# A pair's activations in one run of columns, four single blocks before the second half's weights, and one count of a search step on ScalarE

## The chip, the cores and the metric

The kernel runs as one program on one core of a Trainium2 chip. The metric is device time in microseconds (us). TensorE (PE) multiplies, VectorE (DVE), ScalarE (ACT) and GpSimd (POOL) work elementwise, SyncE (SP) and GpSimd issue the DMAs.

## The reference

Three layers stand one behind the other: attention over pooled keys, a layer with a rational function between two products, and a mixture of eight experts with a greedy assignment. N = 4608 tokens, width 512.

```python
# attention: 8 batches, 8 heads, 576 tokens, width 64; keys and values are means over 8 tokens
k_p, v_p = mean8(k), mean8(v)
x = softmax(q @ k_p.T / 8) @ v_p                 # [4608, 512]
# rational layer, inner width 2048
h = x @ w_in
P = a[0] + a[1]*h + a[2]*h*h + a[3]*h*h*h
Q = 1 + abs(b[0])*abs(h) + abs(b[1])*h*h
y = (P / (Q + 1e-6)) @ w_out                     # [4608, 512]
# experts: all pairs (token, expert) in falling order of their logit; a token takes the first
# expert that still has room (cap = 576)
logits = y @ w_gate
assigned = greedy(logits, cap=576)
for e in range(8):
    out[assigned == e] = relu(y[assigned == e] @ w1[e]) @ w2[e]
```

## The kernel before, in words

All operations are recorded first in an `Order`: each has an engine, an assumed duration, what it reads and writes, and a priority (its place in the recording, or a large negative number for the routing). `Order.run` then plays the list through with these durations and writes out the instructions of each engine in the order that comes of it. So the order on an engine is fixed when the program is built, and an instruction at the head of an engine's queue that waits holds up all behind it.

Every factor of a product is split into a high and a low part (`xh`, `xl`; `wih`, `wil`; `woh`, `wol`; `hi`, `lo`), and each product is three matmuls.

Phase 1 does attention and the rational layer for 18 blocks of 256 tokens. The inner width is worked in two halves of 1024, each in four pieces of 256 (`fp` 0 to 3). In the first half the blocks 0 to 3 go singly (twice, for two pieces each) and the blocks 4 to 17 in pairs; in the second half the blocks 0 and 1 go singly, the rest in pairs. A step is 512 columns of `h`: one pair and 128 inner features, or one block and 256. In a step PE makes `h` (`mm_h`, line 693), ACT and DVE and POOL make the rational function (`act1`, `act2`, lines 708 to 735), and PE multiplies by `w_out` (`mm_y`, lines 791 to 794); the output of 128 tokens gathers over all steps of a part. `hi` and `lo` of a step wait for these products in a ring of buffers `mgl`: five (`mg`), and five more (`mgx`, opened by `swap_m`, closed by `swap_b`) while the first half has pairs.

Attention for the blocks is recorded between the steps. `x` of four blocks lies in SBUF in two tiles, `xt[0]` and `xt[1]`, of [128, block, 4, 256]; a pair's matmul reads two runs of 256 columns, 1024 columns apart. Each block's `x` is stored to DRAM (`store_x`) and loaded again for the second half (`load_b`, line 884, issued on POOL): blocks 0 and 1 into `xt[0]`, which the first half's last pair (16, 17) uses, and blocks 2 and 3 into a new tile `xhr`, `xlr`.

The second half's weights come as 64-bit numbers in 16 parts and are turned into float32 and split (`prep_w`: ACT line 409, DVE 410 to 414, PE 432 and 436, POOL 345). They start when attention is done and its memory is given back (`closed`, from the step after block 15): one part with each step. The tiles of pieces 2 and 3 are those of the first half's pieces 0 and 1, and so are filled once that half is over.

For the last four blocks of the second half the output products are held back (`late`, `DEFER`) and fill PE while the first expert is chosen: 8 groups of 24 matmuls of 512 columns, each followed by ACT line 832 and POOL line 833.

Phase 2 takes the experts one after the other. `route(k)` finds which expert is next and which tokens it takes; its core is `search`, ten steps that narrow a threshold by a factor of four, each with three counts of keys at or above a candidate (`count`, line 1290, DVE), a transpose, a sum and two small operations, all on DVE. Then come gathers on POOL (`fetch`), transposes (`turn`, line 1630) and the expert's two products (`ffn`). `route(0)` stands between the phases; `route(k+1)` runs beside `ffn(k)`.

Of the kernel before, what the change touches and what calls it, by code (L numbers as in the profile page):

```python
# [25 lines left out]
NT = B * S  # L26
DM = H * D
DFF = 2048
E = 8
# [18 lines left out]
GBUFS, MGX, GDX = 5, 5, 5  # L48
# [12 lines left out]
for _name, _width in (("wr", E), ("J", 4), ("sel", E), ("ones", 128), ("qmask", 4), ("cmask", 32), ("own", 2), ("triu", 128), ("s1", 5),  # L61
                      ("tcol", 36), ("pcol", 2), ("rtri", E * E)):
    RC[_name] = (RC.get("n", 0), RC.get("n", 0) + _width)
    RC["n"] = RC[_name][1]
# [15 lines left out]
class Part:  # L80
# [5 lines left out]
    def __call__(self):  # L86
        return self.buf()[:, self.j]

# [202 lines left out]
class Kern:  # L291
# [163 lines left out]
    def init_att(self):  # L455
# [21 lines left out]
        self.xt = [tuple(b(p, [128, 2, 4, BLK], F32R, f"{x}{k}") for x in ("xh", "xl")) for k, p in enumerate(("xp", "xq"))]  # L477
        self.xb = [tuple(Part(x, k % 2) for x in self.xt[k // 2]) for k in range(XBUFS)]
# [201 lines left out]
    def mm_h(self, st):  # L680
# [198 lines left out]
    def load_b(self, n):  # L879

        s, j = n // 2 % 2, n % 2
        extra = [("xr", m) for m in range(NB) if m % XBUFS == j] if n < 2 else []
        for k, x in enumerate(self.x1[s]):
            self.op("Pool", 1.05, lambda k=k, x=x: self.nc.gpsimd.dma_start(x()[:, j], self.x_d[n]()[:, k]), r=[("xd", n, k)],
                    w=[("xs", s, j, k)] + extra, nbytes=524288)

    def phase1(self):
# [4 lines left out]
        for p in ("wp", "mp", "xp", "xq", "ap"):  # L892
# [24 lines left out]
        pieces = {h: [(h, fp, k) for fp in range(NFP) for k in range(4)] for h in range(2)}  # L917
        loads = {h: list(pieces[h]) for h in range(2)}
# [19 lines left out]
        parts = alone + [(0, [n], range(NFP)) for n in range(SPLIT, PAIRS)] + [(0, [n, n + 1], range(NFP)) for n in range(PAIRS, NB, 2)]  # L938
# [11 lines left out]
        for i, st in enumerate(steps):  # L950
            st["i"] = i
            n = st["blk"]
            if st["half"] == 0:
# [4 lines left out]
                if n == SPLIT and st["first"] and st["half"] == 0:  # L958
                    self.swap_m()
                while done < needed[st["blks"][-1]]:  # L960
# [8 lines left out]
                elif not closed and NB - 3 in xdone:  # L969
                    closed = True  # L970
                    reads = [k for k in self.g.lastw if self.in_pool(k, ("ap", "xq"))]
                    reads += [("xr", m) for m in range(NB) if m % XBUFS > 1] + [("x", m, s, k) for m in self.xkeys for s in range(2) for k in self.xkeys[m]]
                    def swap():
                        self.close("ap")
                        self.close("xq")
# [4 lines left out]
                    for fp in range(2):  # L980
                        self.w_tiles(1, fp, "wpb", f"b{fp}")
                        for t in self.w[1, fp]:
                            for k in range(4):
                                self.g.lastw[t, k] = self.g.lastw["swap"]
                    self.staging("raw1")
# [4 lines left out]
                if closed and pieces[1] and pieces[1][0][1] < 2:  # L990
# [3 lines left out]
            else:  # L994
                if st["first"] and n == 0:
# [8 lines left out]
                    for fp in (2, 3):  # L1004
                        self.w[1, fp] = self.w[0, fp - 2]
                while pieces[1] and pieces[1][0][1] <= st["fp"]:
                    piece(1)
# [5 lines left out]
                st["x"] = x if len(st["blks"]) == 2 else tuple(Part(t, n % 2) for t in x)  # L1013
# [81 lines left out]

    def free_x(self, s):
# [3 lines left out]
        new = [tuple(View(x, lambda t, j=j, i=i: t[:, j].rearrange("p (i c) t -> p i (c t)", i=2)[:, i]) for i in range(2))  # L1100
# [5 lines left out]
    def swap_b(self):  # L1106

        def swap():
            self.close("mx")
# [4 lines left out]
        self.op("Z", 0.0, swap, w=[k for k in self.g.lastw if self.in_pool(k, ("wq", "stg", "mx"))] + ["swapb"])  # L1114
        self.mgl = [g for g in self.mgl if g[0].pool != "mx"]
        x = tuple(self.buf("yp", [128, 2, 4, BLK], F32R, x) for x in ("xhr", "xlr"))
        self.x1 = [self.xt[0], x]
        for j in range(2):
            for k in range(2):
                self.g.lastw["xs", 1, j, k] = self.g.lastw["swapb"]  # L1120
# [16 lines left out]
    def swap_g(self):  # L1137
# [5 lines left out]
        self.more_g("gd", "swapg", GDX, "gd")  # L1143
        more = self.ring(MORE_R, "gd", [128, 2 * BLK], F32, "mrg")
# [27 lines left out]
    def init_route(self):  # L1172
# [40 lines left out]
        self.cand, self.thr = b("rt", [128, 4], F32, "cand"), b("rt", [128, 3], F32, "thr")  # L1213
# [73 lines left out]
    def count(self, D, key, cand, col, ck):  # L1287

        j = self.BJ[col % 2]
        D(.43, lambda: self.nc.vector.tensor_scalar(  # L1290
            j(), key(), cand(), None, op0=ALU.is_ge, op1=ALU.add, accum_out=self.cnt()[:, col:col + 1]),
# [22 lines left out]
    def search(self, D, key, col, steps, cap, between=None, sole=None):  # L1314
# [4 lines left out]
        (base, bk), (J, jk) = self.small(0, 4), self.small(4, 4)  # L1319
        D(.07, lambda: V.tensor_scalar(cand(), J(), float(4 ** (steps - 1)), None, op0=ALU.mult), r=[jk], w=[cand])  # L1320
        for i in range(steps):
# [9 lines left out]
            D(.14, lambda Y=Y: V.scalar_tensor_tensor(self.njunk()[:, 0:3], Y()[:, 0:3], cap() if callable(cap) else cap, self.own(3),  # L1331
# [494 lines left out]
```

## Time and profile before

| what | us |
|---|---|
| runs (three), median | 1531.73 (1530.3 to 1533.25) |
| the profiled execution | 1529.58 |
| its span, first to last instruction | 1527.8 |
| PE busy in the span | 1454.1 |
| DVE, ACT, POOL busy | 1097.6, 883.3, 865.0 |

The profile shows one execution. Busy time is the time in which an engine has at least one instruction under way; matmuls overlap, so the distance from one start to the next says more than a matmul's own duration. PEclk and "granted clock" give the share of TensorE's full clock of 2.4 GHz that was granted; 0.5 is its lower level, 1.2 GHz. "Waits" put an engine's idle time down to what ended it.

### The profile page before, as it was taken

What the parts mean: (1) busy time and instruction counts of PE and PEld (TensorE: products, weight loads), DVE (VectorE), ACT (ScalarE), POOL (GpSimd) and SP (SyncE); (2) the same over time, 40 slices, a digit from 0 to 9 for tenths busy, and PEclk for the clock granted to TensorE, in tenths of its full rate; (3) what the DMA queues carried; (4) which work ended last, traced back from release to release, by engine and by line L of the source; (5) the groups of instructions that cost most, each with busy time, mean ns of one, the idle gap of its engine ahead of it and who ended that gap; (6) DMA issues with size and microseconds to landing.
All of it is one profiled execution on the core that took longest, in us unless ns stands there. A gap on an engine that the chain in (4) does not pass through costs nothing. (4 is left out here: it accounts for less than half of the span.)

```text
span 1527.8 us, 27162 instructions
## 1 busy us (share of the span) xinstructions
PE 1454.1 (95%) x9353; PEld 1307.1 (86%) x9353; DVE 1097.6 (72%) x3105; ACT 883.3 (58%) x2071; POOL 865.0 (57%) x806
## 2 busy tenths in 40 slices
PE   8899999999999999989999999995999999999996
PEld 6899978888898998978898998764888988988995
DVE  6897786858768678688777778888788778941220
ACT  5887886867868766656655456841343432443330
POOL 6776877557657456545544455652465554654421
PEclk9999999999999999989999999998999999999998
DMA  6663534132321324523231332003254333433300
GB/s 223 220 226 105 170 123 148 58 130 94 132 102 49 112 73 163 168 82 107 85 103 65 111 108 87 29 29 123 75 172 143 133 114 125 156 114 112 128 18 31
DMA packets 82023, 173.62 MB, mean 114 GB/s; under 512 B 10320, under 2 KB 37328, under 8 KB 81872
## 3 DMA queue, kind: packets, MB, share of 16 engines
q1 hardware_dynamic: 70800, 134.02, 25.9%
q0 software_dynamic: 11072, 37.76, 7.5%
q8 instruction: 74, 1.21, 0.3%
q14 instruction: 77, 0.63, 0.1%
HBM read 122.28 MB, written 49.46 MB: 112 GB/s over the span
## 5 line engine op out<-in xcount | busy, mean ns | idle before, releaser
L345 POOL TENSOR_TENSOR mq<-mq,ms 128x512 f32<-128x512 f32 x144 | 195.1, 1356 | 151.1 <-ACT mq L711 149.2
L693 PE MATMUL pa<-xh,wih 128*128 128x512 f32 (+1 forms) x448 | 166.7, 372 | 4.2 <-ACT wih L351 1.7
L693 PE MATMUL pa<-xh,wil 128*128 128x512 f32 (+1 forms) x448 | 159.3, 356 | 0.8 <-POOL wil L345 0.8
L693 PE MATMUL pa<-xl,wih 128*128 128x512 f32 (+1 forms) x448 | 158.9, 355 | 0.0
L708 ACT ACTIVATE ms<-pa 128x512 f32<-128x512 f32 x144 | 85.8, 596 | 120.1 <-PE pa L693 88.8
L1664 PE MATMUL pa<-yth,w1h 128*128 128x320 f32 (+1 forms) x512 | 145.2, 299 | 1.1 <-ACT yth L1635 0.7
L1664 PE MATMUL pa<-ytl,w1h 128*128 128x320 f32 (+1 forms) x512 | 144.3, 297 | 0.0
L1664 PE MATMUL pa<-yth,w1l 128*128 128x320 f32 (+1 forms) x512 | 143.9, 296 | 0.0
L713 DVE TENSOR_TENSOR mw<-mw,pa 128x512 f32<-128x512 f32 x144 | 97.9, 680 | 54.9 <-ACT mw L709 54.0
L793 PE MATMUL pa<-woh,mg 128*128 128x260 f32 (+1 forms) x484 | 131.1, 293 | 5.0 <-DVE mg L729 2.7
L794 PE MATMUL pa<-wol,mg 128*128 128x260 f32 (+1 forms) x484 | 129.0, 289 | 0.0
L1717 POOL DMA_INDIRECT out<-ob,ix x40 | 38.9, 972 | 152.5 <-ACT ob L1713 130.1
L345 POOL TENSOR_TENSOR mg<-mt,mr 128x512 fp32r<-128x512 f32 x68 | 89.0, 1310 | 63.8 <-DVE mt L733 36.1
L711 ACT ACTIVATE mq<-ms,scal 128x512 f32<-128x512 f32 x144 | 117.8, 818 | 10.0 <-DVE mt L731 9.9
L726 ACT ACTIVATE mr<-mq,scal 128x512 f32<-128x512 f32 x122 | 88.5, 725 | 50.4 <-POOL mq L345 39.5
L709 ACT ACTIVATE mw<-pa,scal 128x512 f32<-128x512 f32 x144 | 112.3, 780 | 1.6 <-PE pa L693 1.2
L1667 ACT ACTIVATE h2h<-pa 128x256 fp32r<-128x256 f32 (+1 forms) x128 | 51.4, 410 | 103.8 <-PE pa L1664 96.9
L565 ACT ACTIVATE ex<-pa,nm 128x72 f32<-128x72 f32 (+2 forms) x320 | 98.5, 325 | 20.0 <-DVE nm L556 13.8
L714 DVE SCALAR_TENSOR_TENSOR pa<-mw,scal,pa 128x512 f32<-128x512 f32 x144 | 107.7, 748 | 3.0 <-ACT ms L708 1.5
L733 DVE SCALAR_TENSOR_TENSOR mt<-pa,scal,mt 128x512 f32<-128x512 f32 x144 | 106.8, 742 | 0.9
L1698 PE MATMUL pa<-w2h,h2h 128*128 128x512 f32 x256 | 102.2, 399 | 0.0
L1290 DVE TENSOR_SCALAR_CACHE_REDUCE BJ<-BQ,cand 128x288 uint16<-128x288 f32 x217 | 99.5, 509 | 3.4 <-ACT BQ L1470 1.5
(325 smaller groups left out, 4865.1 us busy)
## 6 DMA issues: line engine op xcount, KB each, us to landing
wraw<-in_w SPq DMA_DIRECT2D x64, 512.0 KB, 3.6
ya_d<-ya SPq DMA_DIRECT2D x18, 520.0 KB, 3.3
yab<-ya_d SPq DMA_DIRECT2D x18, 520.0 KB, 4.3
kvraw<-in_kT SPq DMA_DIRECT2D x16, 576.0 KB, 4.2
x_d<-xh SPq DMA_DIRECT2D x18, 512.0 KB, 3.4
x_d<-xl SPq DMA_DIRECT2D x18, 512.0 KB, 4.6
y_d<-yb SPq DMA_DIRECT2D x18, 512.0 KB, 3.0
raw<-in_w_in SPq DMA_DIRECT2D x16, 512.0 KB, 4.8
```

What stands on the lines that cost most here:

```text
L345: self.g.either({"Pool": (p_tt(n), lambda: nc.gpsimd.tensor_tensor(out(), x(), y(), op=alu)), "DVE": (c_tt(n), lambda: nc.vector.tensor_te ...
L565: op("Act", c_act(NK, 0, 1, 1), lambda h=h: nc.scalar.activation(e()[:n, h, :], sv()[:, h, :], AF.Exp, bias=nm()[:n, h:h + 1], accum_out=s ...
L693: nc.tensor.matmul(o, w()[:, c, f], x()[:, :, c, :] if two else x()[:, c, :], start=c == 0 and k == 0, stop=c == 3 and k == 2)
L709: op("Act", c_act(N, 0, 2), lambda: nc.scalar.activation(w(), ph(), AF.Identity, scale=self.a3(), bias=self.a2()), r=hk + self.sk, w=[w])
L711: op("Act", c_act(N, 1, 2), lambda: nc.scalar.activation(q(), s(), AF.Identity, scale=self.b1a(), bias=self.b0a()), r=[s] + self.sk, w=[q])
L714: op("DVE", c_stt(N), lambda: nc.vector.scalar_tensor_tensor(ph(), w(), self.a1(), ph(), op0=ALU.add, op1=ALU.mult), r=[w], w=hk)
L733: op("DVE", c_stt(N), lambda: nc.vector.scalar_tensor_tensor(t(), w(), self.a0(), t(), op0=ALU.add, op1=ALU.subtract), r=[(w, 0), self.hri ...
L793: nc.tensor.matmul(o, hi()[:, f], w(woh), start=first, stop=False)
L794: nc.tensor.matmul(o, hi()[:, f], w(wol), start=False, stop=False)
L1290: D(.43, lambda: self.nc.vector.tensor_scalar(j(), key(), cand(), None, op0=ALU.is_ge, op1=ALU.add, accum_out=self.cnt()[:, col:col + 1]), ...
L1664: nc.tensor.matmul(ps()[:, 0:n], w()[:, c, fs], x()[:, c, :], start=i == 0, stop=i == 11)
L1698: nc.tensor.matmul(ps(), x()[:, t], w()[:, f % 2, :], start=f == 0 and i == 0, stop=False)
```

## The change

Four things change together.

- `x` of two blocks lies as [128, 4, block, 256], so a pair's matmul reads 512 columns in one run. A DMA that stores or loads one block's `x` now has, in each partition, four runs of 1 KB in SBUF in place of one of 4 KB.
- In the first half only the blocks 4 to 13 go in pairs; 14 to 17 go singly (`PEND`). Before block 14 what is left of the outputs of 12 and 13 is recorded at once and the five `mgx` buffers are given up (`swap_x`). Both `xt` tiles stay to the end of the phase; the second half's blocks 0 and 1 are loaded into `xt[1]`, which blocks 14 and 15 use, and blocks 2 and 3 into `xt[0]`.
- The second half's weights: piece 2 gets `woh`, `wol` tiles of its own, piece 3 takes those of the first half's piece 0, and the parts that can be made earlier are recorded earlier. When the first half is over, its piece 1's output weights serve as two more pairs of `hi`, `lo` buffers, and three `gd` pairs are opened in place of five.
- In the first nine steps of a `search` the keys below a candidate are counted. Two counts stay on DVE; for the third ACT sums the signs of candidate - 0.5 - key. The comparison with the capacity is turned round to match (`capo`), and one small operation is added at the start of a search.

```diff
-GBUFS, MGX, GDX = 5, 5, 5
+GBUFS, MGX, GDX = 5, 5, 3
...
-        self.xt = [tuple(b(p, [128, 2, 4, BLK], F32R, f"{x}{k}") for x in ("xh", "xl")) for k, p in enumerate(("xp", "xq"))]
-        self.xb = [tuple(Part(x, k % 2) for x in self.xt[k // 2]) for k in range(XBUFS)]
+        self.xt = [tuple(b(p, [128, 4, 2, BLK], F32R, f"{x}{k}") for x in ("xh", "xl")) for k, p in enumerate(("xp", "xp"))]
+        self.xb = [tuple(Col(x, k % 2) for x in self.xt[k // 2]) for k in range(XBUFS)]
...
-            o = ph().rearrange("p (b t) -> p b t", b=2) if two else ph()[:, BLK * j:BLK * j + BLK]
+            o = ph() if two else ph()[:, BLK * j:BLK * j + BLK]
...
-                    nc.tensor.matmul(o, w()[:, c, f], x()[:, :, c, :] if two else x()[:, c, :],
+                    nc.tensor.matmul(o, w()[:, c, f], x()[:, c].rearrange("p b t -> p (b t)") if two else x()[:, c, :],
...
-        extra = [("xr", m) for m in range(NB) if m % XBUFS == j] if n < 2 else []
+        extra = [("xr", m) for m in range(NB) if m % XBUFS == 2 - 2 * s + j] if n < 4 else []
...
+        pieces[1][8:12] = [(1, 2, k) for k in (2, 3, 0, 1)]
...
-        parts = alone + [(0, [n], range(NFP)) for n in range(SPLIT, PAIRS)] + [(0, [n, n + 1], range(NFP)) for n in range(PAIRS, NB, 2)]
+        parts = alone + [(0, [n], range(NFP)) for n in range(SPLIT, PAIRS)] + [(0, [n, n + 1], range(NFP)) for n in range(PAIRS, PEND, 2)]
+        parts += [(0, [n], range(NFP)) for n in range(PEND, NB)]
...
+                if n == PEND and st["first"]:
+                    while rest:
+                        rest.pop(0)()
+                    self.swap_x()
...
-                elif not closed and NB - 3 in xdone:
+                elif not closed and n >= PEND:
...
+                    free = [self.buf("wpb", [128, 2, 2, GW], F32R, f"{x}b2") for x in ("woh", "wol")]
+                    self.w[1, 2] = [*self.w[0, 0][:2], *free]
+                    self.w[1, 3] = [*self.w[0, 1][:2], *self.w[0, 0][2:]]
...
-                if closed and pieces[1] and pieces[1][0][1] < 2:
+                if closed and (len(pieces[1]) > 6 or len(pieces[1]) > 4 and n == NB - 1 and st["fp"] > 0 or len(pieces[1]) > 2 and n == NB - 1 and st["fp"] > 1):
                     piece(1)
...
-        self.x1 = [self.xt[0], x]
+        self.x1 = self.xt[::-1]
...
-    def count(self, D, key, cand, col, ck):
+    def count(self, D, key, cand, col, ck, less=False):
 
-        j = self.BJ[col % 2]
+        j = self.BJ[0 if less else col % 2]
+        if less and col == 2:
+            j = self.BJ[1]
+            self.rop("Act", .52, lambda: self.nc.scalar.activation(
+                j().bitcast(BF16), key(), AF.Sign, scale=-1.0, bias=self.cand()[:, 4:5], accum_out=self.cnt()[:, 2:3]),
+                r=[key, ck], w=[j, (self.cnt, col)])
+            return
...
-            for j in range(n):
-                self.count(D, key, lambda j=j: cand()[:, j:j + 1], j, cand)
+            below = less and not last
+            for j in (2, 0, 1) if below else range(n):
+                self.count(D, key, lambda j=j: cand()[:, j:j + 1], j, cand, below)
...
-PAIRS = SPLIT
+PAIRS, PEND = SPLIT, NB - 4
```

How the order on the engines moves is seen at two places. PE at the end of the first half, before the change: the last `h` products of the pair (16, 17) (tiles `xh`, `xl`, weights `wih`, `wil`) and the first of the output products that follow them.

```order
L693 MATMUL pa_194<-xh_353,wil_1493 128x512
L693 MATMUL pa_194<-xh_353,wih_1472 128x512
L693 MATMUL pa_194<-xl_362,wih_1472 128x512
L693 MATMUL pa_194<-xh_353,wil_1493 128x512
L793 MATMUL pa_233<-woh_291,mg_1460 128x260
L794 MATMUL pa_233<-wol_336,mg_1460 128x260
L791 MATMUL pa_233<-woh_291,mg_1460 128x260
```

Seventy output products of the first half stand there in a row, with only two groups of weight work (lines 432 and 436) among them, before the second half's first `h` product (the weights `wihb`, `wilb`). PE at the same place in the changed kernel:

```order
L700 MATMUL pa_228<-xh_350,wih_1469 128x256
L700 MATMUL pa_228<-xl_359,wih_1469 128x256
L700 MATMUL pa_228<-xh_350,wil_1490 128x256
L439 MATMUL pa_145<-ident,wf_6171 128x128 x4
L700 MATMUL pa_191<-xh_792,wihb_6150 128x256
L700 MATMUL pa_191<-xl_806,wihb_6150 128x256
L700 MATMUL pa_191<-xh_792,wilb_6166 128x256
L700 MATMUL pa_191<-xh_792,wihb_6150 128x256
L700 MATMUL pa_191<-xl_806,wihb_6150 128x256
L700 MATMUL pa_191<-xh_792,wilb_6166 128x256
L800 MATMUL pa_194<-woh_625,mg_1457 128x260
L801 MATMUL pa_194<-wol_656,mg_1457 128x260
```

The second half's products now follow the first half's last `h` at once, and the outputs of the last single block stand among them. ACT in `route(0)`, before the change, from the keys of the search (`BQ`) on; `yb` are outputs of the held-back groups:

```order
L1470 ACTIVATE BQ<-pa_130 128x288
L832 ACTIVATE yb_7460<-pa_270 128x256 x2
L832 ACTIVATE yb_7286<-pa_233 128x256 x2
L832 ACTIVATE yb_7286<-pa_231 128x256 x2
L832 ACTIVATE yb_7460<-pa_274 128x256 x2
L832 ACTIVATE yb_7460<-pa_197 128x256 x2
```

Five groups end after the search has its keys. ACT at the same place in the changed kernel, where `BJ,cnt<-BQ,cand` is the count by signs:

```order
L1503 ACTIVATE BQ<-pa_191 128x288
L1312 ACTIVATE BJ_10866,cnt<-BQ,cand 128x288 x2
L839 ACTIVATE yb_7459<-pa_194 128x256
L1312 ACTIVATE BJ_10866,cnt<-BQ,cand 128x288
L839 ACTIVATE yb_7459<-pa_194 128x256
L1312 ACTIVATE BJ_10866,cnt<-BQ,cand 128x288 x2
L839 ACTIVATE yb_7459<-pa_230 128x256 x2
L1312 ACTIVATE BJ_10866,cnt<-BQ,cand 128x288 x2
L839 ACTIVATE yb_7625<-pa_228 128x256
L1312 ACTIVATE BJ_10866,cnt<-BQ,cand 128x288
L839 ACTIVATE yb_7625<-pa_228 128x256
L1312 ACTIVATE BJ_10866,cnt<-BQ,cand 128x288
```

Nine counts now stand among four groups' outputs, so a count can stand behind an output that waits for PE.

## Rows read from the trace of the kernel before

**Rows 1.** The page, parts 1 and 2: busy time, and slices of 38.2 us.

```profile
PE 1454.1 (95%) x9353; PEld 1307.1 (86%) x9353; DVE 1097.6 (72%) x3105; ACT 883.3 (58%) x2071; POOL 865.0 (57%) x806
...
PEclk9999999999999999989999999998999999999998
```

**Rows 2.** Busy time by stretch (span; PE, PEld, DVE, ACT, POOL; granted clock; DMA).

```profile
590.00:600.00 10.00, 7.09 (x43) 6.30 (x42) 9.59 (x15) 5.09 (x11) 8.14 (x9) 0.83 0.79 252
650.00:660.00 10.00, 6.41 (x24) 5.42 (x25) 9.00 (x15) 8.72 (x16) 6.22 (x7) 0.62 0.53 175
660.00:670.00 10.00, 10.00 (x72) 9.71 (x72) 6.56 (x16) 3.56 (x6) 3.54 (x4) 0.86 0.00 1
700.00:960.00 260.00, 260.00 (x1674) 236.66 (x1673) 201.35 (x439) 145.51 (x225) 133.25 (x116) 1.00 0.29 94
```

**Rows 3.** Waits of PE from 580 to 700 us (total, times, longest).

```profile
PE pa L432 <- DVE wf L414: 2.6, 1, 2.6
PE pa L693 <- ACT wih L351: 1.7, 1, 1.7
PE pa L791 <- POOL mgx L345: 1.6, 1, 1.6
PE pa L436 <- ACT wm L440: 1.3, 1, 1.3
...
PE pa L793 <- DVE mgx L729: 0.8, 1, 0.8
PE pa L693 <- POOL wil L345: 0.8, 1, 0.8
...
```

**Rows 4.** Timeline of PE (start, duration): matmuls of 256 and 512 columns.

```profile
150.31 0.29 PE L693 MATMUL pa<-xl,wih 128*128 128x256 f32 x1
...
151.50 0.28 PE L693 MATMUL pa<-xh,wil 128*128 128x256 f32 x1
...
399.63 0.39 PE L693 MATMUL pa<-xl,wih 128*128 128x512 f32 x1
...
401.96 0.39 PE L693 MATMUL pa<-xh,wil 128*128 128x512 f32 x1
...
1447.69 0.39 PE L1698 MATMUL pa<-w2h,h2l 128*128 128x512 f32 x1
...
1449.78 0.39 PE L1698 MATMUL pa<-w2h,h2h 128*128 128x512 f32 x1
```

**Rows 5.** POOL: the loads of `x`, by line (busy us, mean ns).

```profile
L884 POOL DMA_DIRECT2D xh<-x_d x10 | 5.9, 587 | 0.7 <-PE pa L693 0.7
```

**Rows 6.** Timeline of DVE: first and second count of one step, first of the next.

```profile
1030.38 0.51 DVE L1290 TENSOR_SCALAR_CACHE_REDUCE BJ<-BQ,cand 128x288 uint16<-128x288 f32 x1
...
1030.82 0.51 DVE L1290 TENSOR_SCALAR_CACHE_REDUCE BJ<-BQ,cand 128x288 uint16<-128x288 f32 x1
...
1032.81 0.52 DVE L1290 TENSOR_SCALAR_CACHE_REDUCE BJ<-BQ,cand 128x288 uint16<-128x288 f32 x1
```

**Rows 7.** ACT by line: with and without an accumulator.

```profile
L565 ACT ACTIVATE ex<-pa,nm 128x72 f32<-128x72 f32 (+2 forms) x320 | 98.5, 325 | 20.0 <-DVE nm L556 13.8 <-POOL en L345 5.2 <-POOL vmh L345 0.7
L726 ACT ACTIVATE mr<-mq,scal 128x512 f32<-128x512 f32 x122 | 88.5, 725 | 50.4 <-POOL mq L345 39.5 <-POOL mg L345 8.1 <-POOL mgx L345 2.5
L565 ACT ACTIVATION_READ_ACCUMULATOR ex<-pa,nm 128x1 f32 (+2 forms) x320 | 67.8, 212 | 0.0
```

**Rows 8.** Waits of PE from 1040 to 1075 us.

```profile
PE pa L1630 <- issue: 6.7, 1, 6.7
...
PE pa L1494 <- DVE T L1492: 2.7, 1, 2.7
```

**Rows 9.** Timeline of ACT: the outputs of two held-back groups.

```profile
1039.73 0.66 ACT L832 ACTIVATE yb<-pa 128x256 f32<-128x256 f32 x2 [4.92 <-PE pa L791]
1045.25 0.66 ACT L832 ACTIVATE yb<-pa 128x256 f32<-128x256 f32 x2 [4.86 <-issue]
```

**Rows 10.** Waits of PE from 1100 to 1180 us.

```profile
PE pa L1531 <- DVE S L1530: 2.0, 1, 2.0
...
```

More of the change, by code (lines that the diff above doesn't have):

```diff
@@ L984, in phase1 @@
                                 self.g.lastw[t, k] = self.g.lastw["swap"]
+                    free = [self.buf("wpb", [128, 2, 2, GW], F32R, f"{x}b2") for x in ("woh", "wol")]
+                    self.w[1, 2] = [*self.w[0, 0][:2], *free]
+                    self.w[1, 3] = [*self.w[0, 1][:2], *self.w[0, 0][2:]]
+                    for t in free:
+                        for k in range(4):
+                            self.g.lastw[t, k] = self.g.lastw["swap"]
                     self.staging("raw1")
@@ L1003, in phase1 @@
                         self.load_b(m)
[L1004 to L1007, printed above, removed]
+                    while pieces[1]:
+                        piece(1)
                 if st["first"] and n == SINGLE:
@@ L1099, in free_x @@
         self.op("Z", 0.0, lambda: None, w=[("xs", s, j, k) for j in range(2) for k in range(2)] + [key])
-        new = [tuple(View(x, lambda t, j=j, i=i: t[:, j].rearrange("p (i c) t -> p i (c t)", i=2)[:, i]) for i in range(2))
+        new = [tuple(View(x, lambda t, j=j, i=i: t[:, 2 * j + i].rearrange("p b t -> p (b t)")) for i in range(2))
                for x in self.x1[s] for j in range(2)]
@@ L1108, in swap @@
         def swap():
-            self.close("mx")
             self.close("stg")
@@ L1143, in swap_g @@
         self.more_g("gd", "swapg", GDX, "gd")
+        w = self.w[0, 1][2:]
+        self.op("Z", 0.0, lambda: None, w=[(t, k) for t in w for k in range(4)] + ["freew"])
+        new = [tuple(View(t, lambda t, i=i: t.rearrange("p c g d -> p (c g d)")[:, 512 * i:512 * i + 512]) for i in range(2)) for t in w]
+        for t in (x for g in new for x in g):
+            self.g.lastw[t] = self.g.lastw["freew"]
+        self.mgl = new + self.mgl
         more = self.ring(MORE_R, "gd", [128, 2 * BLK], F32, "mrg")
@@ L1312, in own, with search @@
         return self.c("own").unsqueeze(1).to_broadcast([128, n, 2])
-    def search(self, D, key, col, steps, cap, between=None, sole=None):
+    def search(self, D, key, col, steps, cap, between=None, sole=None, less=False):
         V = self.nc.vector
         thr, cand, nn = self.thr, self.cand, self.nn
-        (base, bk), (J, jk) = self.small(0, 4), self.small(4, 4)
+        (base, bk), (J, jk) = self.small(496, 5), self.small(501, 5)
         D(.07, lambda: V.tensor_scalar(cand(), J(), float(4 ** (steps - 1)), None, op0=ALU.mult), r=[jk], w=[cand])
+        if less:
+            D(.07, lambda: V.tensor_scalar(cand()[:, 4:5], cand()[:, 4:5], -.5, None, op0=ALU.add), w=[cand])
         for i in range(steps):
@@ L1484, in route @@
             so = lambda j: (lambda: self.sole()[:, j:j + 1])
-            self.search(D, BQ, 0, QS, NT / E - .5, rest, so(0))
+            self.search(D, BQ, 0, QS, NT / E - .5, rest, so(0), True)
             D(.1, lambda: self.tc.mark_branch_hint_location(f"settle{k}", engines=[mybir.EngineType.DVE]), r=[(self.thr, 0)], w=[self.flag])
@@ L1783, in host @@
     put("wr", np.tile(8 - r(8), (128, 1)))
-    put("J", np.tile([1, 2, 3, 0], (128, 1)))
+    put("J", np.tile([1, 2, 3, 0, 3], (128, 1)))
+    limit = np.repeat([NT - NT // E + .5] * 2 + [NT - 2 * (NT // E) + 1.0], 2)
+    put("capo", np.where(np.tile(r(128)[:, None] // 16 % 2 == r(2)[None, :], (1, 3)), limit[None, :], -1e6))
     put("sel", r(128)[:, None] == 16 * r(8)[None, :])
```

46 lines of the change are left out of this document (25 added, 21 removed).

## The prediction, made before the changed kernel ran

> **What bounds the kernel now.** I read the page first. Busy shares and the strip of granted clock [rows 1] put PE at 95% of the span, with two dips of the clock, one in the sixteenth to eighteenth slices and a deeper one in the 28th. PE is the bound, so a change pays where PE stands or runs at its lower level, and only there. The table by stretch then says where that is: from 700 to 960 us PE is busy 260 of 260 us [rows 2], so nothing that the other engines do there costs time; from 590 to 670 us, where the halves meet, it stands for 2.9 us of one 10 us stretch and 3.6 us of another, and the clock falls to 0.83, 0.62 and 0.86 of 2.4 GHz. The waits of PE name what it stood for [rows 3]. Third, the start-to-start distances of matmuls [rows 4] give the price of moved PE work, since a duration overlaps the next one. Last come the two engines of the search, DVE's steps [rows 6] and ACT's prices [rows 7, 9], and the waits of PE where a search ends last [rows 8, 10].
>
> **Pairs in one run.** The distance between starts is 0.119 us at 256 columns (ten starts in 1.19 us), 0.233 us at 512 columns in two runs (ten in 2.33) and 0.232 us at 512 columns in one run (nine in 2.09) [rows 4]. So I give the layout 0.0 us on PE; the bounds come with the third rival. Its DMAs have four pieces where they had one. A load costs POOL 587 ns [rows 5]; the bounds for the new form are that price and four times it, 36 loads x 3 x 0.58 = 63 us more of POOL. Most loads fall between 700 and 960 us, where POOL is idle for 260 - 133 = 127 us [rows 2], so even the upper bound stays covered; I take the lower end, which is the nearer row, and 0 us.
> The Trainium skill, page "DMA: Bandwidth & Descriptors", section "SWDGE vs HWDGE vs iDMA", speaks against this edit: software on GpSimd builds a descriptor pair for each operation of a DMA. By it POOL would come near the upper bound; no run here shows it yet, and the sum would still be the same, for the cover just named.
>
> **Four blocks singly.** Two pairs times eight steps times 12 matmuls = 192 matmuls of 512 columns become 384 of 256: 192 x (2 x 0.119 - 0.233) = +1.0 us of PE.
>
> **The meeting of the halves.** Before, 70 output products of the last pair stand alone on PE, behind the elementwise chain. Their waits are those for `mgx` (1.6 and 0.8 us) and for `wm` (1.3 us) [rows 3], and with them goes the clock of 590 to 600 us: 0.83 is 3.4 us at the lower level (17% lost, twice that long), which costs half of it, 1.7 us. After, the second half's products follow at once, so 1.6 + 0.8 + 1.3 + 1.7 = 5.4 us should go. The waits of `h` for `wih` and `wil`, 1.7 + 0.8 = 2.5 us, should go too, since the weight parts stand three steps earlier. The wait for `wf` (2.6 us) lies in the dip of the clock at 650 to 670 us, which is 7.6 + 2.8 = 10.4 us at the lower level [rows 2] and costs between half of (10.4 - 3.6 idle) = 3.4 us and 5.2 us; I take 4.2. Of this 6.8 us I give back half, 3.4 us: the parts of pieces 2 and 3 are still converted in a burst when the first half is over, and ACT and DVE have the work of single blocks beside it. What is late next is the ring: four single blocks run with five pairs of `hi`, `lo` in place of ten, and an output product can wait for its buffer. Its bounds are 0 and the 3.7 us that the end of the half waited before; I take 2.5, since the single blocks issue outputs for one block at a time as the last pair's tail did. Sum: -5.4 - 2.5 - 3.4 + 1.0 + 2.5 = -7.8 us.
>
> **One count by signs.** A step is 1032.81 - 1030.38 = 2.43 us long and its counts are 0.44 us apart [rows 6]; DVE alone makes it, so nine steps lose at most 9 x 0.435 = 3.9 us. ACT's price at 288 columns is not shown: the nearest rows are 325 ns at 72 columns and 725 ns at 512 [rows 7], by a straight line 0.52 us, and 0.21 us to read the accumulator, together 0.73. DVE's two counts take 0.87. So ACT is 0.14 us early if it is free. Between 0.325 and 0.725 for the operation the count comes 0.33 us early or 0.07 us late, a step that saves 0.37 at worst.
> The wait is the larger matter. In the first expert's search ACT also writes the held-back outputs, 5.5 us apart [rows 9], and its queue is in a fixed order. An output that waits for PE holds the sign count behind it, and DVE waits for that. In the order of the changed kernel nine counts stand among six such output instructions; the third and the eighth stand right behind one that PE's group has probably not released yet. I give these 1.0 and 0.85 us, about half a step each, between 0 and a whole step of 2.4. That leaves 3.9 - 1.85 = 2.05 us at my full price and 3.9 at none; I take 2.5. Is it on the path? After the search PE waits 2.7 us for the transposed result `T` and then 6.7 us before the first expert's transposes [rows 8], so all of 2.5 us passes through, and at 2.7 the held-back matmuls would end last instead. The one operation added per search costs about one small operation, 0.2 us at most (the distance from a step's last small operation to its first count), inside the rounding.
> In the second expert's search, beside the first expert's products, PE waits 2.0 us for the slots [rows 10]; at most that goes, and nothing if ACT is as busy with outputs there. I take -1.0. Later searches have no such row, and I give them 0.
>
> **The sum.** -7.8 - 2.5 - 1.0 = -11.3 us. The profiled execution took 1529.58 us, of which 1527.8 are span and 1.8 lie around it; I leave these as they are and get 1518.3. The median of the runs is 1531.73, 2.1 us over the profiled execution, so the forecast is 1520 us. With every term at its good end (-5.4 - 2.5 - 6.8 + 1.0 = -13.7, -3.9, -2.0) it is 1512, with every one at its bad end (the meeting -5.4 - 2.5 + 1.0 + 3.7 = -3.2, the search -0.0, the second search 0) 1528.5. A difference under 0.2%, 3.1 us, is no change that a measurement of this kernel can tell.
>
> **Rival one: the meeting gives nothing.** The weight parts are the same work for DVE and ACT, and DVE is busy 9.6 and 9.0 of 10 us in the two bad stretches [rows 2]. If DVE is what is late there, the stall only moves to other tiles, and half as many ring buffers add to it. Then the search alone counts: 1531.7 + 1.0 - 3.5 = 1529 us. Against it: between 660 and 670 us DVE is down to 6.6 and PE is full, so the load comes in lumps that an earlier start can spread.
>
> **Rival two, slower: the sign counts stick in ACT's queue beside the experts.** The searches of the second to fourth expert run beside an expert's products, with ACT's outputs ahead of a count in the order. PE already waits for the second one [rows 10], so a search that grows pushes PE at once. A step grows once the count waits for more than 1.31 - 0.73 = 0.6 us in ACT's queue (a pair of outputs is 0.66 us [rows 9]). It eats the whole gain of 10.3 us in the other places when 27 steps grow by 0.4 us, so from a wait of 1.0 us a count. At 1.2 us: 27 x 0.62 = 16.7, and 1531.7 - 10.3 + 16.7 = 1538 us. Against it: an output of the experts is seldom blocked for long, as PE gives one every few matmuls.
>
> **Rival three: one run is faster on PE.** 512 columns at 2.4 GHz are 213 ns, and the pairs take 233 [rows 4]. If the break between the two runs costs these 20 ns, 5 pairs x 96 + 8 pairs x 96 = 1248 matmuls give back up to 24 us and the time is 1496 us. Against it stand the expert's products at line 1698, which read one run and take 232 ns.
> The Trainium skill, page "TensorE: Matmul & The Clock Gate", section "Wait — 56ns, not 53.3ns?", gives 215.7 ns for 512 columns at the full level whatever the source; by that figure the gain would be 1248 x 0.017 = 21 us. The trace disagrees: 232 ns in either layout.
>
> **Chances.** Forecast 0.65, rival one 0.21, rival two 0.11, rival three 0.03. The forecast's own range is 1512 to 1528. The range of 8 in 10 reaches to 1531, which takes in rival one, and down to 1510, since the lower end of the meeting could also win small gaps that I didn't price; both other rivals stay out. Faster: 0.61 of the forecast's 0.65, 0.08 of rival one's 0.21 and rival three make 0.72. Same: 0.03 + 0.11 + 0.01 = 0.15. Slower: the rest, 0.13.
>
> **What would show it.** In the trace after: no output products alone between the halves, no wait for `wih` there, and a clock of 1.00 around 590 us (first term); a wait for `wf` about half as long (second); waits for `mg` in the last four blocks of under 3 us (ring); a step of about 2.0 us on DVE with two steps of about 3 us, where ACT's output stands ahead of the count (search); the wait for the slots in the second expert at about 1 us. The prediction is wrong if PE's idle time between 480 and 700 us is as large as before, if a step beside the experts is longer than before, or if the pairs' starts are no longer 0.233 us apart.

## The result and the profile after

The changed kernel takes 1506.64 us (median of four runs, 1502.17 to 1507.55), the kernel before 1532.4 beside it: a ratio of 0.983 (95% interval 0.981 to 0.985), 25.8 us faster. Two later sets gave 1509.1 us (0.985, 0.982 to 0.988) and 1507.02 us (0.983, 0.982 to 0.985). The forecast was 1520 us with a range down to 1510; the direction was right and the size less than half of what came.

The profiled execution took 1502.17 us, with a span of 1500.4 us, 27.4 less than before. The page, parts 1 and 2, of the changed kernel (busy time; granted clock in slices of 37.5 us):

```profile
PE 1446.0 (96%) x9545; PEld 1309.1 (87%) x9545; DVE 1075.6 (72%) x2986; ACT 914.5 (61%) x2197; POOL 872.8 (58%) x806
...
PEclk9999999999999999999999999997999999999999
```

Of the two dips of the clock in [rows 1] the first is gone. To see where 27.4 us went, I put marks at four instructions that both kernels have. The timeline of PE before, start and duration: the first `h` product of block 14, the last `h` product of the second half, and the first product of an expert; then the same three after.

```profile
491.31 0.50 PE L693 MATMUL pa<-xh,wih 128*128 128x512 f32 x1
...
1001.97 0.39 PE L693 MATMUL pa<-xh,wil 128*128 128x512 f32 x1
...
1072.47 0.58 PE L1664 MATMUL pa<-yth,w1h 128*128 128x256 f32 x1 [0.69 <-ACT yth L1635]
```

```profile
486.62 0.39 PE L700 MATMUL pa<-xh,wih 128*128 128x256 f32 x1
...
981.74 0.40 PE L700 MATMUL pa<-xh,wil 128*128 128x512 f32 x1
...
1051.47 0.58 PE L1697 MATMUL pa<-yth,w1h 128*128 128x256 f32 x1 [0.69 <-ACT yth L1668]
```

The last work of the program is POOL's issue of the last output, before and then after:

```profile
1516.52 0.90 POOL L1717 DMA_INDIRECT out<-ob,ix  x1 [3.42 <-DVE ob L1716]
```

```profile
1496.49 0.90 POOL L1750 DMA_INDIRECT out<-ob,ix  x1 [3.42 <-DVE ob L1749]
```

| stretch | before | after | won |
|---|---|---|---|
| start to the first `h` product of block 14 | 491.3 | 486.6 | 4.7 |
| to the last `h` product | 510.7 | 495.1 | 15.5 |
| to the first expert's first product (the first choice) | 70.5 | 69.7 | 0.8 |
| to the end of the last output's issue | 445.0 | 445.9 | -0.9 |
| from there to the end of the span | 10.4 | 3.0 | 7.4 |

Ahead of block 14 PE has the same 3301 matmuls in the same order in both kernels, and that mark stands at 486.6, 489.1 and 490.6 us in three profiles of the changed kernel and at 488.8 to 494.0 in the nine kernels below that are the one before with one edit each; so I put the 4.7 us of the first row to scatter. Two things stand out that the forecast did not have: the second row is large, and 7.4 us were won after all the work is done. The table by stretch, in the columns of [rows 2], of the changed kernel:

```profile
590.00:600.00 10.00, 10.00 (x87) 10.00 (x86) 9.48 (x17) 8.79 (x16) 6.28 (x6) 1.00 0.18 56
650.00:660.00 10.00, 8.85 (x63) 7.85 (x62) 9.31 (x31) 3.41 (x5) 3.14 (x3) 1.00 0.31 107
660.00:670.00 10.00, 10.00 (x58) 8.72 (x58) 7.32 (x21) 4.40 (x7) 2.58 (x2) 1.00 0.34 107
```

and the waits of PE from 580 to 700 us, all of them:

```profile
PE pa L1296 <- DVE ext L1294: 1.1, 1, 1.1
PE pa L800 <- DVE wf L421: 0.9, 1, 0.9
PE pa L800 <- DVE mt L740: 0.4, 1, 0.4
```

Against [rows 3] the waits for `mgx`, `wm`, `wih` and `wil` are gone, that for `wf` is a third, and none for the ring's `mg` came. The clock stays at 1.00 throughout. For all kernels below I count what PE lost there as the stretch from the first `h` product of block 14 to the last `h` product, less the sum over its matmuls of their usual start-to-start distances (0.232 us at 512 columns, 0.119 at 256, 0.120 at 260, and the median of both traces for the rest): 20.0 us before, 3.3 after, so 16.7 less. In six profiles of the changed kernel and its variants in the search it is 3.3 to 3.4 us; in the seven kernels below that change only the count, the run of columns or the pieces of the loads in the kernel before it is 21.6 to 25.9, so the profile of before stands at the low end.

The end of the program is in the instructions that close it, listed by line, engine queue and operation (count; shortest, median and longest ns; first and last start). Before, and after:

```profile
L1822 POOLq DRAIN  x3: 46/107/10685, 1516.3 to 1527.5; - x3
```

```profile
L1857 POOLq DRAIN  x3: 46/107/3337, 1496.3 to 1500.1; - x3
```

The longest DRAIN of POOL's queue starts 0.2 us ahead of the last output's issue. It lasts 10.69 us before and 3.34 after, and the span ends 0.8 us behind it in both. The last output lands 2.6 us from the start of its issue in both, so the drain goes on for 7.9 us behind the last data before the change and for 0.5 after.

The search of the first expert, DVE, the first counts of two steps, and ACT's count by line (busy, mean ns):

```profile
1010.65 0.51 DVE L1316 TENSOR_SCALAR_CACHE_REDUCE BJ<-BQ,cand 128x288 uint16<-128x288 f32 x1
...
1011.21 0.51 DVE L1316 TENSOR_SCALAR_CACHE_REDUCE BJ<-BQ,cand 128x288 uint16<-128x288 f32 x1
...
1012.84 0.51 DVE L1316 TENSOR_SCALAR_CACHE_REDUCE BJ<-BQ,cand 128x288 uint16<-128x288 f32 x1
```

```profile
L1312 ACT ACTIVATE BJ<-BQ,cand 128x288 bf16<-128x288 f32 x63 | 33.6, 533 | 36.1 <-DVE cand L1367 35.5
L1312 ACT ACTIVATION_READ_ACCUMULATOR BJ<-BQ,cand 128x1 f32 x63 | 11.9, 188 | 0.0
```

A step is 2.19 us, where [rows 6] had 2.43: 0.24 less, not 0.435. The two counts now start 0.56 us apart and not 0.44, since the order puts the step's small operation between them, and behind the second the transpose has nothing to hide the accumulator's read. ACT's count was priced well: 0.53 us, and 0.19 to read.

### The profile page after: what moved, and what is told of

Its sections match the earlier page's. It is cut to its first block, busy times and chain, and to the rows that moved or that the text cites. A ratio compares the mean times of both kernels' runs of the same rounds, so it can differ in the third digit from the quotient of the medians.

```text
span 1500.4 us, 27509 instructions
## 1 busy us (share of the span) xinstructions
PE 1446.0 (96%) x9545; PEld 1309.1 (87%) x9545; DVE 1075.6 (72%) x2986; ACT 914.5 (61%) x2197; POOL 872.8 (58%) x806
## 3 DMA queue, kind: packets, MB, share of 16 engines
q0 software_dynamic: 24896, 37.76, 9.0%
## 5 line engine op out<-in xcount | busy, mean ns | idle before, releaser
L700 PE MATMUL pa<-xh,wih 128*128 128x256 f32 (+1 forms) x576 | 202.0, 351 | 2.5 <-ACT ex L572 1.2
L700 PE MATMUL pa<-xh,wil 128*128 128x256 f32 (+1 forms) x576 | 195.3, 339 | 0.0
L700 PE MATMUL pa<-xl,wih 128*128 128x256 f32 (+1 forms) x576 | 194.7, 338 | 0.0
L1697 PE MATMUL pa<-ytl,w1h 128*128 128x256 f32 (+1 forms) x512 | 144.4, 298 | 0.0
L1697 PE MATMUL pa<-yth,w1l 128*128 128x256 f32 (+1 forms) x512 | 143.9, 296 | 0.0
L352 POOL TENSOR_TENSOR mg<-mt,mr 128x512 fp32r<-128x512 f32 x78 | 101.0, 1295 | 69.9 <-DVE mt L740 37.8
L700 PEld LDWEIGHTS pa<-xh,wih 128*128 128x128 f32 x576 | 109.0, 189 | 14.1 <-ACT ex L572 2.0
L700 PEld LDWEIGHTS pa<-xh,wil 128*128 128x128 f32 x576 | 108.7, 189 | 12.6
L700 PEld LDWEIGHTS pa<-xl,wih 128*128 128x128 f32 x576 | 109.1, 189 | 9.0
```

The lines of the kernel that those rows point to most:

```text
L352: self.g.either({"Pool": (p_tt(n), lambda: nc.gpsimd.tensor_tensor(out(), x(), y(), op=alu)), "DVE": (c_tt(n), lambda: nc.vector.tensor_te ...
L700: nc.tensor.matmul(o, w()[:, c, f], x()[:, c].rearrange("p b t -> p (b t)") if two else x()[:, c, :], start=c == 0 and k == 0, stop=c == 3 ...
L1697: nc.tensor.matmul(ps()[:, 0:n], w()[:, c, fs], x()[:, c, :], start=i == 0, stop=i == 11)
```

## The experiments

All ratios are to the kernel before, timed on the same chip. The searches first. Three counts on DVE again, in the changed kernel:

```diff
-            self.search(D, BQ, 0, QS, NT / E - .5, rest, so(0), True)
+            self.search(D, BQ, 0, QS, NT / E - .5, rest, so(0))
```

> The changed kernel with all three counts of a search step on VectorE again. Theory (the sign count is worth its shorter step wherever a search ends last): the first choice gets 9 x 0.235 = 2.1 us longer, the later searches some 0.5 us a step in places, in sum 5 to 8 us slower than the changed kernel (about 1513 us). Rival (only the first choice is on the path): 2 us slower (about 1508.5). If the count by signs cost as much as it saved, no difference.

Measured 1511.12 us, ratio 0.986 (0.983 to 0.989). Beside it the changed kernel once more:

> The changed kernel once more, beside the variants of this set. Its first profile lost 27.4 us against the kernel before: by milestones on PE 1.5 before the first pair, 18.7 between there and the end of the second half, 1.5 in the first expert's choice and 6 behind it. Theory: all of that is the change, so the ratio to the kernel before is 0.983 again and the stretch behind the first choice is again about 6 us shorter. Rival: the first profile was a lucky one (1502 against 1507 in the other runs), and the 6 us behind the first choice shrink to 2 or 3.

It gave 0.985 (0.982 to 0.988). The difference of 2 us is the rival's, though the intervals overlap. The profile of this second execution has 446.7 us from the first expert's product to the last issue, where the kernel before has 445.0: nothing is won behind the first choice. I had taken the shorter drain for it. The count alone, on the kernel before (all of `count`, `search`, `capo` and the call with `True`, and nothing else of the change):

> The kernel before with one edit: the count by signs on ScalarE. Theory: it gives what its removal takes from the changed kernel, 5 to 8 us (about 1526). Rival: 2 us, the first choice alone (about 1530).

1533.28 us, ratio 1.000 (0.998 to 1.002): neither. In its profile the first choice is 1.3 us shorter than before (69.2 in place of 70.5), but the last `h` product comes 4.2 us later (1006.2). Last, DVE's second count got an output buffer of its own, so that the small operation moves behind it:

```diff
-        self.BJ = self.ring(2, "rt", [128, 288], U16, "BJ")
+        self.BJ = self.ring(3, "rt", [128, 288], U16, "BJ")
...
-        j = self.BJ[0 if less else col % 2]
+        j = self.BJ[2 * (col % 2) if less else col % 2]
```

> The changed kernel with a third output buffer for the counts, so that VectorE's second count does not follow the first one's write and the small operation between them moves behind it, beside the wait for the accumulator. Theory: a step goes from 2.20 to 2.00 us, the first choice gets 1.8 us shorter, and later searches as much where they end last: 2 to 4 us faster than the changed kernel. Rival: TensorE is the bound there by now, no difference.

> The changed kernel with a third output buffer for the counts once more, now beside the changed kernel on the same chip: 1 to 2 us faster than that, or, if TensorE is the bound behind the search, the same within 1.5 us.

> The changed kernel beside it: ratio to the kernel before 0.983 to 0.985.

1507.4 us (0.984) in one set; in the other 1506.81 us (0.984, 0.982 to 0.985) beside 1507.02 for the changed kernel. A step fell to 2.07 us, and the time did not. PE's wait for `T` fell from 2.3 us to 1.2, but the wait behind it, for `S`, grew by 0.6; why is not shown. The waits of PE around the choice, changed kernel and this one:

```profile
PE pa L1663 <- issue: 6.9, 1, 6.9
PE pa L1564 <- DVE S L1563: 3.8, 1, 3.8
PE pa L1586 <- DVE Sel L1580: 3.3, 1, 3.3
PE pa L1527 <- DVE T L1525: 2.3, 1, 2.3
...
```

```profile
PE pa L1663 <- issue: 6.9, 1, 6.9
PE pa L1564 <- DVE S L1563: 4.4, 1, 4.4
PE pa L1586 <- DVE Sel L1580: 3.3, 1, 3.3
PE pa L1527 <- DVE T L1525: 1.2, 1, 1.2
...
```

Now the layout, alone on the kernel before (the change's edits of `xt`, `Col`, `mm_h` and `load_b`, and the views that follow from them).

> The kernel before with one edit: x of a pair in one run of 512 columns, with DMAs of 1 KB runs. Theory: 512 columns start 0.232 us apart in either layout, so no change (within 1.5 us of the kernel before). Rival: one run is faster on PE, up to 20 us less; or the shorter DMA runs cost time, slower by 2 us or more.

1524.67 us, ratio 0.995 (0.993 to 0.997): 7.1 us faster, though the last `h` product comes no earlier (1004.5 us) and the issue of the last output ends at 1520.4 us, 3.0 later than before. The drain is 3.33 us. So the layout wins its time after the work, and I split it: the kernel before with its two-run layout for PE, but pieces of 1 KB in the loads.

```diff
-        self.x_d = [b("drm", [128, 2, 4, BLK], F32, f"x_d{n}") for n in range(NB)]
+        self.x_d = [b("drm", [128, 2, 4, 320], F32, f"x_d{n}") for n in range(NB)]
...
-self.nc.gpsimd.dma_start(x()[:, j], self.x_d[n]()[:, k])
+self.nc.gpsimd.dma_start(x()[:, j], self.x_d[n]()[:, k, :, 0:256])
```

> The kernel before with one edit: in DRAM a block's x lies with a gap behind each 1 KB, so a load or store of it is made of four pieces of 1 KB a partition, as in the changed kernel; in SBUF, and for TensorE, everything stays as before (two runs of 256 columns). The kernel with the layout alone was 7.1 us faster, and its trace shows the last drain of GpSimd's queue at 3.33 us in place of 10.69, with all work ending no earlier. Theory P (the pieces of the loads that GpSimd issues set that drain): 3.3 us of drain and about 7 us faster than before. Rival L (the layout that TensorE reads gives it): 10.7 us and no change.

1524.42 us, ratio 0.995 (0.993 to 0.996), drain 3.34: theory P. PE's reading plays no part. The next five change only how many pieces GpSimd's queue gets, by the gaps (two rows of 512 + 64 elements, eight of 128 + 32, or rows of 256 + 64 for the first blocks alone), or by taking the loads to SyncE's queue:

```diff
-            self.op("Pool", 1.05, lambda k=k, x=x: self.nc.gpsimd.dma_start(x()[:, j], self.x_d[n]()[:, k]), ...
+            self.dma(lambda x=x: x().bitcast(F32)[:, j], lambda k=k: self.x_d[n]()[:, k], 524288, ...
```

> The kernel before with one edit: the second half's x is loaded by SyncE's queue in place of GpSimd's, in whole 4 KB runs. Theory P1 (the long drain belongs to direct loads of long runs on GpSimd): drain 3.3 us, 7 us faster. Theory P2 (the drain is longer the fewer pieces GpSimd's queue has had): drain 10.7 us or longer, no faster. The loads stand in another queue's order, so some us either way between the halves.

> As the kernel with four pieces a partition, but with two of 2 KB. If the drain falls steadily with the pieces, it lies between 3.3 and 10.7 us, near 8. If it depends on what is left over in a ring after the last wrap, it can be anything, above 10.7 too. If only pieces over 2 KB matter, 3.3.

> As the kernel with four pieces a partition, but with eight of 512 B. A steady fall or a threshold: 3.3 us, the floor, since the last output lands 2.7 us after its issue. A ring's remainder: it can be above 3.3 us. GpSimd's issue of a load, 0.58 us with one piece and 0.79 with four, shows about 1.1 us.

> The kernel before, with four pieces of 1 KB only in the eight loads of the blocks 0 to 3 (14144 packets in GpSimd's queue in place of 11072). So far the last drain took 7.75 us at 5888 packets, 10.69 at 11072, 4.40 at 15680, 3.34 at 24896 and 5.95 at 43328. Theory R (the drain works off what was issued since a ring last came round, so it counts the packets, at 0.57 us per 1000 from the first two): 12.4 us if the ring has not come round by 14144, else under 4.4. Rival F (the form of the loads sets it, long runs being slow): a little under 10.7, as 28 of 36 loads are as before.

> The same with the twelve loads of the blocks 0 to 5: 15680 packets, as many as with two pieces in every load. Theory R, by the number of packets alone: 4.4 us, as there. Rival F: about 9 us, between the two forms.

The page's third part counts the packets of that queue; the drain is from each trace:

| kernel | packets | drain, us | time, us |
|---|---|---|---|
| loads by SyncE | 5888 | 7.75 | 1525.87 |
| before | 11072 | 10.69 | 1531.7 |
| four pieces in 8 of the loads | 14144 | 3.95 | 1525.82 (one run) |
| two pieces in every load | 15680 | 4.40 | 1524.55 (one run) |
| four pieces in 12 of the loads | 15680 | 4.40 | 1527.62 (one run) |
| four pieces in every load | 24896 | 3.34 | 1524.42 |
| eight pieces in every load | 43328 | 5.95 | 1529.75 (one run) |

The lines of the two kernels with 15680 packets, the two pieces first:

```profile
L1822 POOLq DRAIN  x3: 46/107/4397, 1517.6 to 1522.5; - x3
```

```profile
L1822 POOLq DRAIN  x3: 46/107/4397, 1520.6 to 1525.6; - x3
```

Two forms of load with one count of packets give the same drain to the nanosecond, and the drain goes up, down and up again with the count. So here the count sets it and not the form (rival F expected 9 us), and it may be a remainder, of what has been issued since something last came round; that is not shown. The Trainium skill, page "DMA: Bandwidth & Descriptors", section "Terms", says that descriptors of GpSimd's DMAs are written to rings in SBUF, which fits; no run shows the ring itself. The rule stays open: from 5888 to 11072 the slope is 0.57 us per 1000 packets, from 14144 to 15680 it is 0.29. The kernel with SyncE's loads also has 36 DMAs fewer in that queue, so its 7.75 us, which neither P1 nor P2 expected, need not come of the packets alone; of the 5.8 us that it is faster the drain gives 2.9, and at the meeting of the halves its PE loses 17.1 us. In eight pieces the issue of a load took 0.92 us, not the 1.1 expected.

The meeting of the halves. Late weights in the changed kernel:

```diff
-                if closed and (len(pieces[1]) > 6 or len(pieces[1]) > 4 and n == NB - 1 and st["fp"] > 0 or len(pieces[1]) > 2 and n == NB - 1 and st["fp"] > 1):
+                if closed and len(pieces[1]) > 8:
...
-                    while pieces[1]:
-                        piece(1)
+                while pieces[1] and pieces[1][0][1] <= st["fp"]:
+                    piece(1)
```

> The changed kernel, but only the first 8 of the 16 weight parts of the second half are recorded in the first half, one with each step, and the other 8 when a step first needs them, as before the change; tiles, single blocks and loads of x stay. Theory A (the early weights are what empties the meeting of the halves): the waits for wf and wih and the dip of the clock come back, 7 to 9 us slower than the changed kernel (about 1515). Theory B (the single blocks and the early x do it, since PE always has products to put in between): within 2 us of the changed kernel.

1518.91 us, ratio 0.992 (0.989 to 0.994), 9.8 us slower than the changed kernel beside it: theory A. PE loses 16.6 us from block 14 to the last `h` product in place of 3.4 (second profile of the changed kernel), and the waits for `wih`, `wf` and `wil` are back, from 560 to 700 us:

```profile
PE pa L700 <- ACT wih L358: 3.1, 2, 2.9
PE pa L439 <- DVE wf L421: 2.6, 1, 2.6
PE pa L700 <- POOL wil L352: 2.4, 2, 1.5
...
```

The `x` of the second half's first blocks late:

```diff
-        extra = [("xr", m) for m in range(NB) if m % XBUFS == 2 - 2 * s + j] if n < 4 else []
+        extra = [("xr", m) for m in range(NB) if m % XBUFS == 2 * s + j] if n < 4 else []
...
-        self.x1 = self.xt[::-1]
+        self.x1 = list(self.xt)
```

> The changed kernel, but the second half's blocks 0 and 1 are loaded into the x tile that the last blocks 16 and 17 use, and blocks 2 and 3 into the other one: their x comes only when block 16, and block 17, are through. Theory (the kernel before stood on 70 output products alone because the x of its second half could not come while the last pair ran): PE waits for x when the halves meet, 4 to 6 us slower than the changed kernel (about 1512). Rival (with single blocks half of x is free four steps earlier, and outputs fill the rest): under 1.5 us.

1511.26 us, ratio 0.986 (0.983 to 0.989), about 2 us by the ratios; PE loses 6.3 us, and one wait is new (`PE pa L700 <- DMA xl<-x_d`, 1.9 us). Between theory and rival. Both together (the 12 and 5 us that the text below names are 13.2 and 3.0 when counted from block 14 on, as here):

> The changed kernel with both edits at once: weights as late as before the change, and the x of the second half's first blocks into the tile that is used last. Alone, the first loses 9.8 us and the second 2.2 (12 and 5 us in the profiles). Theory (these two carry the gain where the halves meet, the single blocks themselves give nothing): TensorE loses about 21 us between 480 us and the end of the second half, as before the change, and the time is 1521 us. Rival (they overlap: while PE waits for the weights, x comes): no slower than with late weights alone, 1519.

1521.42 us, ratio 0.992 (0.989 to 0.995). PE loses 18.7 us, near the 20.0 of before. By time alone it can't be told from late weights alone. Then the single blocks, alone on the kernel before:

```diff
-        parts = alone + [(0, [n], range(NFP)) for n in range(SPLIT, PAIRS)] + [(0, [n, n + 1], range(NFP)) for n in range(PAIRS, NB, 2)]
+        parts = alone + [(0, [n], range(NFP)) for n in range(SPLIT, PAIRS)] + [(0, [n, n + 1], range(NFP)) for n in range(PAIRS, PEND, 2)]
+        parts += [(0, [n], range(NFP)) for n in range(PEND, NB)]
```

> The kernel before with one edit: the first half's blocks 14 to 17 go singly (ten buffers, weights and x as before). Theory A (the pairs' long tail of outputs is what stands alone when the halves meet): the drain goes, 5.4 - 1.0 and part of the weight waits, 6 to 10 us faster (about 1524). Theory B (the late weights and x hold the second half back): within 2 us of the kernel before.

1535.16 us, ratio 1.002 (1.000 to 1.003): theory B, they give nothing and may cost 2.5 us. PE loses 19.4 us. And half of them in the changed kernel:

```diff
-PAIRS, PEND = SPLIT, NB - 4
+PAIRS, PEND = SPLIT, NB - 2
```

> The changed kernel with two single blocks last (16, 17) in place of four; the ring is cut to five and the weights' memory opened at block 16, so the weight parts start four steps later. Theory (early weights carry the gain, and the four single blocks are there to open their memory early): 4 to 8 us slower than the changed kernel. Rival (two singles do as well): within 1.5 us.

1529.72 us, ratio 0.998 (0.997 to 1.000): some 20 us slower than the changed kernel, far more than I expected. PE loses 24.4 us; the drain is still 3.34 us. The waits of PE from 560 to 720 us:

```profile
PE pa L700 <- DVE mt L740: 3.8, 2, 3.2
PE pa L700 <- ACT wih L358: 3.8, 1, 3.8
PE pa L800 <- DVE mg L736: 2.3, 1, 2.3
PE pa L700 <- POOL wil L352: 2.1, 2, 1.6
PE pa L798 <- POOL mg L352: 1.3, 1, 1.3
...
```

With two single blocks the ring is cut and the weights' memory opened one pair later: the first weight part starts on ACT at 562.8 us in place of 525.6 and the last at 650.5 in place of 624.3, and the short ring waits beside them. The start of the last part, counted from the first `h` product of block 14, goes with what PE loses in all these kernels: 138 to 140 us where it loses 3.3 to 6.3 (the changed kernel, late `x`), 156 to 161 where it loses 16.6 to 24.4 (before, late weights, both, four and two single blocks). The single blocks are worth what they make room for.

## Why the prediction was wrong

**The meeting of the halves, mis-sized.** Forecast -8.8 us of lost time (-7.8 with the 1.0 for the single matmuls), measured 20.0 - 3.3 = 16.7 us less lost on PE. The mechanism was the one named, and its first two terms (-5.4 and -2.5) came in full: no wait for `mgx`, `wm`, `wih` or `wil` is left. Two terms failed. "Of this 6.8 us I give back half": the wait for `wf` kept 0.9 of 2.6 us and the clock of that stretch never fell, so about 6 of 6.8 us went. The burst that I gave it back for is still there, but it is over sooner: six parts still come behind the second half's first `h` product (eight before), and the last of the 16 starts on ACT 138 us behind the first `h` product of block 14 in place of 158. Before, and after:

```profile
648.97 0.69 ACT L409 ACTIVATE wm<-raw 128x512 f32<-128x512 f32 x1
```

```profile
624.26 0.68 ACT L416 ACTIVATE wm<-raw 128x512 f32<-128x512 f32 x1
```

And "an output product can wait for its buffer ... I take 2.5": the lower bound held, with no wait for `mg` from 580 to 700 us. These two make 5.0 of the 7.9 us that were missed. The other 2.9 had no term, since the terms held only 14.7 of the 20.0 us that PE lost there: 1.6 are two waits of PE before, from 580 to 700 us, that [rows 3] leaves out, and they are gone too; the rest are small gaps:

```profile
PE pa L793 <- DVE mg L729: 0.8, 1, 0.8
PE pa L791 <- POOL gd L345: 0.8, 1, 0.8
```

Rival one is refuted: DVE is as busy as before (9.48 and 9.31 of 10 us in the stretches above), and PE waits for it for 2.4 us in all from 580 to 700 us.

**The pairs in one run, right on PE and wrong at the end.** "So I give the layout 0.0 us on PE" holds: the kernel with that edit alone ends its second half no earlier, and starts stay 0.23 us apart. Rival three is refuted. That the 20 ns over 213 come with the type of the numbers is suggested, though not shown, at 256 columns: in the trace of before bf16 matmuls (the fillers of line 331, `idle`) start 0.109 us apart there, the products 0.119. For the DMAs I bounded POOL's time from both sides, and the issue of a load did go from 0.58 to only 0.79 us [rows 5], hidden as named. The line of after, with mean ns:

```profile
L891 POOL DMA_DIRECT2D xl<-x_d x18 | 14.2, 791 | 0.0
```

What failed is that "a load costs POOL" was its whole price. The step left out the 10.4 us behind the last issue, in which no engine computes: I took the span's end for the end of work, and so put the pieces' effect there at nothing without a reason; it was 7.4 us. The row that would have asked the question was in the trace of before, a DRAIN of 10.69 us against a last output that lands within 3 us of its issue. It would not have given the size, as no row of before shows another count of packets.

**The count by signs, right in kind, too large in size.** Forecast -2.5 for the first choice, measured -0.8 between the marks, and about 2 us by the runs without it. The wait that I feared in ACT's queue did not come: DVE waits for no count there, and all steps are 2.19 to 2.20 us. "Nine steps lose at most 9 x 0.435" was a bound, but the step's small operation and the accumulator's read had been hidden behind the third count, and 0.2 us of each step came back. That leaves 9 x 0.24 = 2.2 us, of which 0.8 arrived: the search's first count came 0.7 us later behind the last `h` product (26.0 us before, 26.7 after), and from the end of `T` to the expert's first product it took 0.6 us more (19.1, 19.7). The second term, -1.0 for the second expert, shows as 0.4 us at the wait for the slots (2.0 before [rows 10], 1.6 after), and the stretch as a whole is no shorter. Rival two did not happen: the first nine steps of the six later searches take 22.5 to 28.9 us in all, 24.5 to 30.3 before, though single steps grew (the ninth of the third search from 3.3 to 6.8 us). The wait for the slots, from 1078 to 1160 us after the change:

```profile
PE pa L1564 <- DVE S L1563: 1.6, 1, 1.6
```

**The basis.** The profiled execution of the changed kernel was 4.5 us under its median, where that of before was 2.1 us under. Three profiles of the changed kernel have spans of 1500.4, 1503.5 and 1505.7 us, and 4.0 of these 5.3 us lie ahead of block 14: the profiled execution was lucky there, by scatter and not by the change.

In sum: 16.7 where the halves meet, 7.4 in the drain and 0.8 in the choice make 24.9, less 1.2 for the matmuls of 256 columns (192 x 0.006; forecast 1.0) and 0.9 among the experts. With the 4.7 us of scatter ahead of block 14 that is the 27.4 of the two spans, to 0.1. The medians differ by 25.8 us: beside the other profiles, the one of the changed kernel was lucky ahead of block 14, and the one of before where the halves meet.

## What to carry to other kernels

Account for the whole span before adding up edits: mark the last work, and ask what each queue does behind it. When a stall has several causes in a row (a buffer, a weight part, an input), size the gain from what the engine lost there by start-to-start distances, between two instructions that both kernels have, and look for what opens the memory that lets the early work start; an edit that gives nothing alone can be the key to the one that does. Before a count of operations is taken off a chain, look which of its neighbours were hidden behind it.

## What was not expected of the hardware

The closing DRAIN of GpSimd's queue takes between 3.3 and 10.7 us, the same to within some 20 ns in all kernels with the same packets (10.685 us in three of them, 3.33 to 3.35 in twelve), and it changes with the number of packets without a steady direction. At 3.34 us, about the least seen, it spans the last output's issue (0.90 us) and landing (2.7 us from issue).
